# A two-layer attention and token-mixer kernel: the value column's ones on ScalarE, queries in front of keys, and three mixer rows in two parts

## The chip, the cores and the metric

One Trainium2 chip, of which the kernel uses one core. The metric is the device time of one execution in microseconds (us); smaller is better.

## What is computed

```python
x = A_x                                                        # 2048 tokens, D = 640
x = x + _A_ref(_layernorm(x), A_wqkv, A_wo)                    # layer 0: attention, 32 heads of 20
x = x + _B_ref(_layernorm(x), B_w1, B_b1, B_w2, B_b2)          # layer 0: token mixer
x = x + _A_ref(_layernorm(x), A_wqkv, A_wo)                    # layer 1, same weights
x = x + _B_ref(_layernorm(x), B_w1, B_b1, B_w2, B_b2)

# _A_ref: q, k, v = x @ wqkv; softmax(q k^T / sqrt(20)) v; @ wo
# _B_ref: u = gelu(einsum("bsd,sf->bdf", h, w1) + b1); y = einsum("bdf,fs->bds", u, w2) + b2
```

The mixer multiplies over the tokens: its first matrix w1 is 2048 x 1536, so every one of the 1536 rows of u needs all 2048 normalised tokens.

## The kernel before

**Tiles.** The 2048 tokens are 16 tiles of 128. Queries go in four blocks of 512 (tb or qb 0 to 3), heads in eight groups of four (g 0 to 7). Scores S are matmuls into PSUM (L703); ScalarE turns two or three banks of them at a time into exponentials P (L773), which is most of its work; PE multiplies P by the values (L1326, into acc). Vaug holds the values of each head with one more column of ones, so that the same matmul gives the softmax's sum; the column is written once, in layer 0's start (L1546, a VectorE memset of 128 x 512; the neighbouring padding is zeroed by ScalarE, L1544 to L1549). A part of the exponentials is worked out on VectorE (L563, L593, L597, L614, L616, with scores in the bank Dt and results in Pd), with steps of it on GpSimd (POOL: L661, L644).

**The order.** The program is written out by a planner in Python that runs when the kernel is built: `attention()` keeps an estimated clock for each engine, puts in score groups, attention x value matmuls and, in the room that is left on PE, fills, and the chip then runs each engine's instructions in this fixed order. A fill is a small group of matmuls with a priority (lowest first), and a step that empties its PSUM bank (misc or Dt): T transposes a normalised tile into hh (L1225, emptied at L366 on ScalarE or L370 on VectorE), V makes values (L1201), K and Q project keys and queries of one head group and one token block (L1177, emptied at L370 and L372), y is the mixer's second matmul of the layer in front (L1685, emptied at L1668), O the output projection (L1117), M the mixer's first matmul (L1068). Where no fill is there, matmuls of zeros stand (L762).

**Priorities in layer 1's front.** K of token block tb must come before the scores that use it; the four Q fills of block 1 follow with priority base[1] + 12 + 8g, behind K of their head groups.

**The mixer's first matmul.** The sum over token tiles is split into two groups, tiles 0 to 7 and 8 to 13; the last two tiles come at the end (um, L1753). `enqueue_mm1_partial` puts in, for each of the 12 rows ft of 128 features, two fills (columns 0 to 319 and 320 to 639) of eight or six matmuls. The first group's result goes by L1081 to ustg and by a DMA from POOL's queue to uacc in memory. For the second group (`direct`) `fetch_row` brings that row back (L1035) into buffers that have come free (three rows in a query buffer QTq, four in hh, five in KT), and L1076 adds the bank to it. The weight tile w1st of a row is loaded one row ahead (L1047, two buffers). The second group is put in when all of its tiles are normalised (`after` in `do_ln2`).

**The end of a layer.** `attention()` makes the rest of the attention x value matmuls, empties at most some fills into `tail_banks`, and calls `end_tiles`: residuals are copied into PSUM (L955), the gelu table is loaded (L956), the last output projection is added (L960), leftover fills follow, then the statistics and normalisation of tiles 14 and 15 (L980 to L999), then um. For layer 0 the next layer's front follows, for layer 1 the output tiles.

**The start of layer 0** (`TokenFeed.begin`). Tiles of x are loaded and normalised on VectorE (L886, L889, L893, L901, L907, with a power on POOL at L903), transposed, and copied on ScalarE (L366); ScalarE also copies the projection weights from w_raw into padded form (L1559).

Of the kernel before, what the change touches and what calls it, by code (L numbers as in the profile page):

```python
# [81 lines left out]
def kernel(  # L82
# [141 lines left out]
    def attention(st, x_in_ap, x_mid, uacc_l, feed, feed_stack):  # L224
# [705 lines left out]
        def do_ln2(tt, x1s, end):  # L930
            def dst():
                if tt >= IN_HH:
                    assert check_hT_dead()
                    h2_tiles[tt] = h2_view[:, tt, :]
                else:
                    assert len(vready) == 2 * NT
                    h2_tiles[tt] = h2_low[:, tt, :]
                return h2_tiles[tt]

            def after(e):  # L940
                ln_open.remove(tt)
                p = next(i for i, grp in enumerate(M_GROUPS) if tt in grp)
                if all(i in h2_tiles for i in M_GROUPS[p]):
                    enqueue_mm1_partial(p, e + DVE_TO_PE)
            ln_open.append(tt)
            ln_proc(x1s[:], True, dst, 3, end + DVE_NEXT, after)
# [74 lines left out]
        def fetch_row(ft):  # L1021
            if ft >= NF or ft in fetched:
                return
# [18 lines left out]

        def mm1_prefetch(p, ft):
            if ft < NF and (p, ft) not in w1_of:
                group = M_GROUPS[p]
                w1st = w1_of[(p, ft)] = late["w1sp"].tile([128, max(map(len, M_GROUPS)), 128], BF16, name="w1st")
                nc.sync.dma_start(out=w1st[:, 0:len(group), :],  # L1047
                                  in_=B_w1[group[0] * 128:(group[-1] + 1) * 128, ft * 128:(ft + 1) * 128].rearrange(
                                      "(a s) f -> s a f", s=128))

        def enqueue_mm1_partial(p, ready):
            group = M_GROUPS[p]
            rows_in = [h2_tiles[tt] for tt in group]
            n_in = len(group)
            direct = p == len(M_GROUPS) - 1
            rows = {}
            sent = {}

            mm1_prefetch(p, 0)
            for ft in range(NF):  # L1060
                for ci, (c0, c1) in enumerate(((0, D // 2), (D // 2, D))):
                    w = c1 - c0
                    mms = []
                    for sti in range(n_in):
                        def mm(t, sti=sti, ft=ft, c0=c0, c1=c1, w=w, ci=ci):
                            if sti == 0 and ci == 0:
                                mm1_prefetch(p, ft + 1)
                            pe(nc.tensor.matmul(t[:, 0:w], lhsT=w1_of[(p, ft)][:, sti, :],  # L1068
                                                rhs=rows_in[sti][:, c0:c1], start=(sti == 0), stop=(sti == n_in - 1)))
                            low_left[0] -= not direct and sti == n_in - 1  # L1070
                        mms.append(mm)
# [65 lines left out]
        def enqueue_outproj_last(half, pairs, ready):  # L1137
# [3 lines left out]
            if half == 0:  # L1141
                mm1_prefetch(1, 0)
                for ft in range(4):
                    fetch_row(ft)
# [72 lines left out]
        def t_fill(tt, h_bf, ready, done):  # L1217
# [15 lines left out]
            def after(end):  # L1233
# [3 lines left out]
                if all(4 * tb + i in tready for i in range(4)):  # L1237
# [9 lines left out]
                    if tb in EQ and tb > 0:  # L1247
                        for g in range(EG):
                            proj_fill("Q", g, tb, base[tb] + 16.0 + 8.0 * g - 4, at, fed=True)
                if len(tready) == NT and NQB > 1:  # L1250
# [24 lines left out]
        def fill_step(alloc=None):  # L1275
# [11 lines left out]
            if fs["idx"] == len(grp["mms"]):  # L1287
                t, bank = fs["tile"], fs["bank"]
                fs["cur"] = None
                eng = evac_engine() if grp["act"] else dvm  # L1290

# [161 lines left out]
        for t in sums:  # L1453
            zero_wave(t[:, 0:512], True, True)
            zero_wave(t[:, 512:D], True, True, HALF / 2, D - 512)
        tail_banks = [sums[0][:, 1024:1536], None, None]

        def tail_alloc():
            bank = tail_banks.pop()
            return bank if bank is not None else Dbank.alloc() if len(tail_banks) == 1 else misc.alloc()  # L1460
        room = pem["t"] + 1.3
# [9 lines left out]
    class TokenFeed:  # L1471
        groups = 4
        early_qbs = (0, 1)
        ve_early = True
        act_helps = True
        act_free = 0.0
# [29 lines left out]
        def begin(self, cx):  # L1506
# [36 lines left out]
            def zero_values(e):  # L1543
                nc.scalar.memzero(Vv[:, :, :, DH:VW])  # L1544
                nc.scalar.memzero(Vv[:, :, 4 * self.groups, 0:32 - VW])
                cx.submit(cx.Proc(2.6, [(0.49, lambda e: nc.vector.memset(Vv[:, :, :, DH:DH + 1], 1.0), 0.0)], e + 5.0))  # L1546
            cx.submit(cx.Proc(1.4, [(1.35, zero_values, -0.06),
                                    (0.2, lambda e: nc.scalar.memzero(Vaug[:, NKT * H * VW:]), -0.06)] +
                              [(1.0, lambda e, i=i: nc.scalar.memzero(pads(i, 1)), -0.06) for i in range(2)],  # L1549
                              2.1, eng=cx.acm))  # L1550

            def group_copy(i, g):
# [10 lines left out]
                def done(e):  # L1563
                    cx.w_at[(i, g)] = e + 0.05
                    self.second -= g >= self.groups
                ready = 22.0 if g >= self.groups else 11.0 if g else (6.2, 7.5)[i]
                cx.submit(cx.Proc((0 if g == 0 else 1.5) if g < self.groups else 5, [(0.5, copied, 0.0)], ready, eng=eng, after=done))
            for g in range(NG):
# [24 lines left out]
    class MixFeed:  # L1593
        groups = 4
        early_qbs = (0, 1)
        ve_early = False
        act_helps = True
        act_free = 0.0
# [284 lines left out]
```

## Time and profile before

| what | us |
|---|---|
| median of 3 runs (1754.08 to 1754.12) | 1754.12 |
| the profiled execution | 1754.05 |
| its span on the core | 1752.3 |
| first exponential starts | 15.97 |
| layer 0's last exponential ends, layer 1's first starts | 816.82, 853.26 |
| layer 1's last exponential ends | 1681.39 |

The span is the time from the first to the last recorded instruction. A timeline row gives start and duration in us, engine, line, operation, and in brackets the idle time before it and what ended it. A windows row gives a stretch, its length, the busy time with instruction count of each engine (or of one line), the granted clock as a share of full speed, the busy share of the DMA engines, and GB/s. A group row gives busy us, mean ns of one instruction, and the idle time in front. SP issues most of the DMAs, in order.

### The profile page before, as it was taken

To read this page: it belongs to the slowest core of one execution; us is meant where nothing else is said; L and a number is where in the kernel's file an instruction comes from. 1 tells how busy PE (TensorE), PEld (TensorE's weight loads), DVE (VectorE), ACT (ScalarE), POOL (GpSimd) and SP (SyncE) were. 2 spreads that over 40 slices of the span, in tenths; PEclk is the share of its full clock that TensorE was granted. 3 is DMA by queue.
4 is the path that set the end of the run, shared out by engine and by line. 5 is a ranking of instruction groups with operands and counts; after the bars stand their busy time and mean duration, and the time that the engine had idled before them with its cause. 6 is when DMAs were issued, how large, how long until landed. Compare 5 with 4: busy or idle time off the path is not lost.

```text
span 1752.3 us, 43289 instructions
## 1 busy us (share of the span) xinstructions
PE 1677.7 (96%) x17891; PEld 663.4 (38%) x17891; DVE 1534.9 (88%) x2491; ACT 1665.0 (95%) x1498; POOL 592.0 (34%) x936
## 2 busy tenths in 40 slices
PE   8999999999999999999999999999999999999999
PEld 3333333333333344444434433233333333444455
DVE  7789999999999999998543469999999999999973
ACT  8999999999999999999779999999999999999970
POOL 2243443353544343332000023434434443434310
PEclk9999999999999999999999999999999999999999
DMA  4020000000122010133322100001001220101445
GB/s 117 9 24 10 1 2 2 24 24 2 35 66 82 25 47 3 39 97 97 125 69 75 65 11 1 1 2 43 20 2 61 82 76 6 62 3 40 120 122 178
DMA packets 103014, 81.87 MB, mean 47 GB/s; under 512 B 50976, under 2 KB 87456, under 8 KB 102816
## 3 DMA queue, kind: packets, MB, share of 16 engines
q1 hardware_dynamic: 97280, 71.22, 13.5%
q0 software_dynamic: 5536, 7.88, 1.5%
q8 instruction: 140, 2.29, 0.5%
q14 instruction: 58, 0.48, 0.1%
HBM read 55.48 MB, written 23.59 MB: 45 GB/s over the span
## 4 chain that ended last, share of the span: by engine, by line
ACT 50%; PE 25%; issue 22%; DVE 2%; DMA 1%; POOL 0%; SPq 0%; ACTq 0%; DVEq 0%
ACT P L773 50%; PE S L703 7%; PE acc L1326 4%; PE misc L1068 2%; PE ya L1766 2%; PE misc L1177 2%; PE acc L762 2%; PE um L1753 1%; PE Dt L1177 1%; PE ya L1775 1%; PE yb L1766 1%; DMA w2s<-in_B_w_dram 1%; PE misc L1117 0%; PE misc L1685 0%; PE misc L1201 0%
## 5 line engine op out<-in xcount | busy, mean ns | idle before, releaser
L773 ACT ACTIVATE P<-S 128x1536 bf16<-128x1536 f32 (+1 forms) x1430 | 1617.4, 1369 | 13.5 <-PE S L703 13.0
L703 PE MATMUL S<-QTq,KT 32*128 32x512 bf16 (+1 forms) x4449 | 575.6, 337 | 60.9 <-ACT P L773 44.4
L661 POOL TENSOR_SCALAR ey<-ew 128x512 f16<-128x512 uint16 x516 | 320.6, 621 | 689.6 <-DVE et L597 306.4
L703 PEld LDWEIGHTS <-KT 32*128 32x128 bf16 x5127 | 229.6, 91 | 524.6 <-issue 497.0
L563 DVE TENSOR_SCALAR ew<-Dt 128x512 int32<-128x512 f32 x524 | 357.0, 681 | 22.3 <-PE Dt L703 14.8
L1326 PE MATMUL acc<-P,Vaug 128*32 128x512 bf16 (+1 forms) x4442 | 363.3, 343 | 0.3 <-DVE Vaug L370 0.3
L762 PE MATMUL acc<-zr,zw 128*32 128x512 bf16 x4256 | 328.1, 382 | 1.2 <-POOL zr L155 1.2
L597 DVE SCALAR_TENSOR_TENSOR et<-ey,ew 128x1024 int16<-128x1024 f16 x262 | 325.6, 1243 | 2.8
L644 POOL TENSOR_SCALAR Pd<-ew 128x512 int16<-128x512 int16 x317 | 196.8, 627 | 161.6 <-DVE et L597 42.4
L703 PE MATMUL Dt<-QTq,KT 32*128 32x512 bf16 (+1 forms) x678 | 201.4, 333 | 0.0
L593 DVE TENSOR_TENSOR ey<-ey 128x1024 f16<-128x1024 f16 x262 | 188.3, 719 | 1.4 <-POOL ey L661 0.3
L1326 PEld LDWEIGHTS <-Vaug 128*32 128x32 bf16 x5120 | 102.7, 94 | 175.4 <-issue 161.4
L762 PEld LDWEIGHTS <-zw 128*32 128x32 bf16 x4476 | 111.5, 96 | 97.9 <-issue 52.5
L616 DVE SCALAR_TENSOR_TENSOR Pd<-ew,et 128x1024 int16<-128x1024 int16 (+1 forms) x134 | 134.6, 1005 | 0.6
L614 DVE TENSOR_TENSOR Pd<-Pd,et 128x1024 int16<-128x1024 int16 (+1 forms) x189 | 121.8, 645 | 5.8 <-POOL Pd L644 3.8
L903 POOL TENSOR_TENSOR rstd<-veps,mhalf 128x1 f32<-128x1 f32 x60 | 49.4, 824 | 224.6 <-DVE veps L901 197.2
L1326 PE MATMUL acc<-Pd,Vaug 128*32 128x512 bf16 (+1 forms) x678 | 102.9, 336 | 1.4 <-DVE Pd L614 1.2
L1177 PE MATMUL misc<-hh,wq_pad 128*128 128x512 bf16 x290 | 84.0, 383 | 0.0
L1068 PEld LDWEIGHTS <-w1st 128*128 128x128 bf16 x672 | 52.9, 97 | 58.2 <-issue 45.3
L1177 PE MATMUL misc<-hh,wk_pad 128*128 128x512 bf16 x255 | 74.0, 383 | 0.0
L1068 PE MATMUL misc<-x1last,w1st 128*128 128x320 bf16 x384 | 73.0, 302 | 0.0
L1117 PE MATMUL misc<-wo_pad,attnT 128*128 128x320 bf16 x384 | 72.3, 302 | 0.2 <-DVE xin L1129 0.2
(145 smaller groups left out, 1180.4 us busy)
## 6 DMA issues: line engine op xcount, KB each, us to landing
w2s<-in_B_w_dram SPq DMA_DIRECT2D x16, 768.0 KB
uacc<-ustg POOLq DMA_DIRECT2D x24, 320.0 KB, 2.6
x1in<-xd SPq DMA_DIRECT2D x24, 320.0 KB
w1st<-in_B_w_dram SPq DMA_DIRECT2D x24, 256.0 KB
xd<-x2s SPq DMA_DIRECT2D x16, 320.0 KB
xin<-xd SPq DMA_DIRECT2D x16, 320.0 KB
w1st<-in_B_w_dram SPq DMA_DIRECT2D x24, 192.0 KB
xd<-x1s SPq DMA_DIRECT2D x12, 320.0 KB
```

Of the source, the lines that this page charges most:

```text
L563: nc.vector.tensor_scalar(out=w[:, slot, :], in0=Dt[:, :], scalar1=127.0 * FIX, scalar2=0.0, op0=ALU.add, op1=ALU.max)
L593: nc.vector.tensor_tensor(out=y, in0=y, in1=y, op=ALU.mult)
L597: nc.vector.scalar_tensor_tensor(out=box["t"][:, 0:512 * k], in0=ve_y.pop(p)[:, 0:512 * k], scalar=MANT_C * MANT_K ** 2, in1=frac, op0=ALU ...
L616: nc.vector.scalar_tensor_tensor(out=bits, in0=whole[:, lo:hi], scalar=128.0, in1=t, op0=ALU.mult, op1=ALU.add)
L644: after_vector(nc.gpsimd.tensor_scalar(out=bits, in0=whole, scalar1=128.0, scalar2=0.0, op0=ALU.mult, op1=ALU.add))
L661: return engine.tensor_scalar(out=out_ap, in0=in_ap, scalar1=MANT_K / FIX, scalar2=-MANT_K * MANT_S, op0=ALU.mult, op1=ALU.add)
L703: pe(nc.tensor.matmul(out_ap[:, c0:c0 + w], lhsT=KT[32 * j:32 * j + 32, g, kt * 128:(kt + 1) * 128], rhs=get_QT(st, qb)[32 * j:32 * j + 32 ...
L762: pe(nc.tensor.matmul(bank[32 * j:32 * j + 32, 0:w], lhsT=zw[:], rhs=zr[:, :, 0:64].to_broadcast([128, w // 64, 64]), start=start, stop=st ...
L773: nc.scalar.activation(out=P[:, 0:ncs, :].rearrange("p a b -> p (a b)"), in_=St[:, 0:ncs, :].rearrange("p a b -> p (a b)"), func=ACT.Exp, ...
L1068: pe(nc.tensor.matmul(t[:, 0:w], lhsT=w1_of[(p, ft)][:, sti, :], rhs=rows_in[sti][:, c0:c1], start=(sti == 0), stop=(sti == n_in - 1)))
L1177: pe(nc.tensor.matmul(t[:, :], lhsT=wpad[:, dt_, g, :], rhs=hT[:, dt_, tb * 512:(tb + 1) * 512], start=(dt_ == 0), stop=(dt_ == NDT - 1)))
L1326: pe(nc.tensor.matmul(acc[32 * j:32 * j + 32, a0:a0 + w], lhsT=Vaug[:, (kt * H + hh_) * VW:(kt * H + hh_) * VW + 32], rhs=P[:, slot, c0:c0 ...
```

## The change

Five edits. (1) In layer 0's start the ones of the value column are no longer a VectorE memset: ScalarE runs an ACTIVATE (identity with bias 1) over the column that it has just zeroed, between its own clearings; the planner's numbers for the pads and the weight copies change with it, and the copies of transposed tiles 0 to 3 are fixed to ScalarE (`act_evacs`). ScalarE's order becomes: zeros, ones, pads, copies of tiles 0 and 1, first key weights, tile 2, first query weights, tile 3, the other six weight copies (before: key weights, tile 0, query weights, tiles 1 to 3, six weight copies). (2) In layer 1 (`early_q`) the four query fills of block 1 get priority base[1] - 5.5, in front of that block's keys. (3) In layer 1 (`mid_rows = 3`) the second mixer group is put in as three parts: rows 0 to 2 with tiles 8 to 11 as soon as these exist, rows 3 to 11 with all six tiles, then rows 0 to 2 with tiles 12 and 13. That makes six more additions (L1076) and three more loads of w1st; the number of matmuls is the same. Layer 0 keeps one part. (4) `tail_alloc` goes round the banks misc, Dt and a score bank, and empties a waiting bank before it is used again. (5) `fetch_row` may not skip a row.

```diff
@@ -939,9 +939,13 @@
 
             def after(e):
                 ln_open.remove(tt)
-                p = next(i for i, grp in enumerate(M_GROUPS) if tt in grp)
-                if all(i in h2_tiles for i in M_GROUPS[p]):
-                    enqueue_mm1_partial(p, e + DVE_TO_PE)
+                if tt < IN_HH and all(i in h2_tiles for i in M_GROUPS[0]):
+                    enqueue_mm1(0, M_GROUPS[0], range(NF), e + DVE_TO_PE)
+                if IN_HH <= tt < 4 * LASTQB and feed.mid_rows and all(i in h2_tiles for i in M_GROUPS[1][:4]):
+                    enqueue_mm1(1, M_GROUPS[1][:4], range(feed.mid_rows), e + DVE_TO_PE)
+                if tt >= IN_HH and all(i in h2_tiles for i in M_GROUPS[1]):
+                    enqueue_mm1(2, M_GROUPS[1], range(feed.mid_rows, NF), e + DVE_TO_PE)
+                    enqueue_mm1(3, M_GROUPS[1][4:], range(feed.mid_rows), e + DVE_TO_PE)
             ln_open.append(tt)
             ln_proc(x1s[:], True, dst, 3, end + DVE_NEXT, after)
 
@@ -1019,7 +1023,7 @@
             return cursor[0] >= n
 
         def fetch_row(ft):
-            if ft >= NF or ft in fetched:
+            if ft >= NF or ft in fetched or ft > len(st.ua):
                 return
             if ft == len(st.ua):
                 if ft == 0:
@@ -1040,31 +1044,34 @@
                 fetch_row(ft + k)
             return ft in fetched and fetched[ft] <= pem["t"]
 
-        def mm1_prefetch(p, ft):
-            if ft < NF and (p, ft) not in w1_of:
-                group = M_GROUPS[p]
+        def mm1_prefetch(p, group, ft):
+            if (p, ft) not in w1_of:
                 w1st = w1_of[(p, ft)] = late["w1sp"].tile([128, max(map(len, M_GROUPS)), 128], BF16, name="w1st")
                 nc.sync.dma_start(out=w1st[:, 0:len(group), :],
                                   in_=B_w1[group[0] * 128:(group[-1] + 1) * 128, ft * 128:(ft + 1) * 128].rearrange(
                                       "(a s) f -> s a f", s=128))
 
-        def enqueue_mm1_partial(p, ready):
-            group = M_GROUPS[p]
+        def enqueue_mm1(p, group, fts, ready):
             rows_in = [h2_tiles[tt] for tt in group]
             n_in = len(group)
-            direct = p == len(M_GROUPS) - 1
+            direct = p > 0
             rows = {}
             sent = {}
-
-            mm1_prefetch(p, 0)
-            for ft in range(NF):
+            fts = list(fts)
+            if fts and p < 3:
+                mm1_prefetch(p, group, fts[0])
+            for fi, ft in enumerate(fts):
                 for ci, (c0, c1) in enumerate(((0, D // 2), (D // 2, D))):
                     w = c1 - c0
                     mms = []
                     for sti in range(n_in):
-                        def mm(t, sti=sti, ft=ft, c0=c0, c1=c1, w=w, ci=ci):
+                        def mm(t, sti=sti, fi=fi, ft=ft, c0=c0, c1=c1, w=w, ci=ci):
                             if sti == 0 and ci == 0:
-                                mm1_prefetch(p, ft + 1)
+                                mm1_prefetch(p, group, ft)
+                                if fi + 1 < len(fts):
+                                    mm1_prefetch(p, group, fts[fi + 1])
+                                elif p == 2 and feed.mid_rows:
+                                    mm1_prefetch(3, M_GROUPS[1][4:], 0)
                             pe(nc.tensor.matmul(t[:, 0:w], lhsT=w1_of[(p, ft)][:, sti, :],
                                                 rhs=rows_in[sti][:, c0:c1], start=(sti == 0), stop=(sti == n_in - 1)))
                             low_left[0] -= not direct and sti == n_in - 1
@@ -1139,7 +1146,7 @@
             tt0 = 4 * LASTQB + 2 * half
             load_xin(tt0)
             if half == 0:
-                mm1_prefetch(1, 0)
+                mm1_prefetch(2, M_GROUPS[1], feed.mid_rows)
                 for ft in range(4):
                     fetch_row(ft)
             for ttl in range(2):
@@ -1246,7 +1253,8 @@
                                       gate=feed.gate_late if g >= EG else None, fed=g < EG)
                     if tb in EQ and tb > 0:
                         for g in range(EG):
-                            proj_fill("Q", g, tb, base[tb] + 16.0 + 8.0 * g - 4, at, fed=True)
+                            proj_fill("Q", g, tb, base[tb] + (8.0 * g + 12.0 if feed.early_q is None else 0.01 * g + feed.early_q),
+                                      at, fed=True)
                 if len(tready) == NT and NQB > 1:
                     enqueue_qproj(1)
             add_fill(("T", tt), when(0, tb) - 6 + 0.1 * (tt % 4), mms, evac, D, ready=ready, after=after, wave=0.1,
@@ -1287,7 +1295,7 @@
             if fs["idx"] == len(grp["mms"]):
                 t, bank = fs["tile"], fs["bank"]
                 fs["cur"] = None
-                eng = evac_engine() if grp["act"] else dvm
+                eng = dvm if not grp["act"] else acm if grp["key"] in feed.act_evacs else evac_engine()
 
                 def emptied(end):
                     grp["evac"](t, end, eng)
@@ -1453,11 +1461,14 @@
         for t in sums:
             zero_wave(t[:, 0:512], True, True)
             zero_wave(t[:, 512:D], True, True, HALF / 2, D - 512)
-        tail_banks = [sums[0][:, 1024:1536], None, None]
+        tail_banks = [misc.alloc, Dbank.alloc, lambda: sums[0][:, 1024:1536]]
+        tail_used = [0]
 
         def tail_alloc():
-            bank = tail_banks.pop()
-            return bank if bank is not None else Dbank.alloc() if len(tail_banks) == 1 else misc.alloc()
+            if tail_used[0] >= len(tail_banks) and len(held) > 1:
+                force(held.pop(1))
+            tail_used[0] += 1
+            return tail_banks[(tail_used[0] - 1) % len(tail_banks)]()
         room = pem["t"] + 1.3
         while fs["cur"] is not None or (fill_queue and pem["t"] < room):
             fill_step(tail_alloc)
@@ -1472,6 +1483,9 @@
         groups = 4
         early_qbs = (0, 1)
         ve_early = True
+        act_evacs = [("T", tt) for tt in range(4)]
+        mid_rows = 0
+        early_q = None
         act_helps = True
         act_free = 0.0
         warm_until = 5.6
@@ -1543,10 +1557,11 @@
             def zero_values(e):
                 nc.scalar.memzero(Vv[:, :, :, DH:VW])
                 nc.scalar.memzero(Vv[:, :, 4 * self.groups, 0:32 - VW])
-                cx.submit(cx.Proc(2.6, [(0.49, lambda e: nc.vector.memset(Vv[:, :, :, DH:DH + 1], 1.0), 0.0)], e + 5.0))
             cx.submit(cx.Proc(1.4, [(1.35, zero_values, -0.06),
                                     (0.2, lambda e: nc.scalar.memzero(Vaug[:, NKT * H * VW:]), -0.06)] +
-                              [(1.0, lambda e, i=i: nc.scalar.memzero(pads(i, 1)), -0.06) for i in range(2)],
+                              [(0.55, lambda e: nc.scalar.activation(out=Vv[:, :, :, DH:DH + 1], in_=Vv[:, :, :, DH:DH + 1],
+                                                                     func=ACT.Identity, bias=1.0, scale=1.0), -0.06)] +
+                              [(0.5, lambda e, i=i: nc.scalar.memzero(pads(i, 1)), -0.06) for i in range(2)],
                               2.1, eng=cx.acm))
 
             def group_copy(i, g):
@@ -1563,8 +1578,8 @@
                 def done(e):
                     cx.w_at[(i, g)] = e + 0.05
                     self.second -= g >= self.groups
-                ready = 22.0 if g >= self.groups else 11.0 if g else (6.2, 7.5)[i]
-                cx.submit(cx.Proc((0 if g == 0 else 1.5) if g < self.groups else 5, [(0.5, copied, 0.0)], ready, eng=eng, after=done))
+                ready = 22.0 if g >= self.groups else 11.5 if g else (7.5, 8.7)[i]
+                cx.submit(cx.Proc((1.2 if g == 0 else 1.5) if g < self.groups else 5, [(0.5, copied, 0.0)], ready, eng=eng, after=done))
             for g in range(NG):
                 for i in range(2):
                     group_copy(i, g)
@@ -1592,8 +1607,11 @@
 
     class MixFeed:
         groups = 4
+        act_evacs = ()
         early_qbs = (0, 1)
         ve_early = False
+        mid_rows = 3
+        early_q = -5.5
         act_helps = True
         act_free = 0.0
         warm_until = 0.0
```

## The prediction

> **What bounds the kernel now.** I read the page first, then the windows of the exponentials' line alone, then the timelines around the holes. On the page a busy row gives us, share and count; a group's row gives busy us, mean ns, then idle time and its releaser.
>
> ```profile
> span 1752.3 us, 43289 instructions
> PE 1677.7 (96%) x17891; PEld 663.4 (38%) x17891; DVE 1534.9 (88%) x2491; ACT 1665.0 (95%) x1498; POOL 592.0 (34%) x936
> L773 ACT ACTIVATE P<-S 128x1536 bf16<-128x1536 f32 (+1 forms) x1430 | 1617.4, 1369 | 13.5 <-PE S L703 13.0
> ```
>
> PE has the larger share, but part of it is L762, which multiplies zeros; the exponentials wait only 13.5 us in all. Windows of L773 (stretch, its length, busy us) and ScalarE's timeline (start, us):
>
> ```profile
> 15.97:816.82 800.85, 800.28 (x707) 1.00 0.12 32
> 853.26:1681.39 828.13, 817.11 (x723) 1.00 0.13 40
> 1681.39:1752.30 70.91, 0.01 (x1) 1.00 0.59 182
> ```
>
> ```profile
> 883.44 7.37 ACT L773 ACTIVATE P<-S 128x1024 bf16<-128x1024 f32 x7 [8.34 <-PE S L703]
> 892.16 7.38 ACT L773 ACTIVATE P<-S 128x1536 bf16<-128x1536 f32 x7 [1.35 <-PE S L703]
> 900.59 6.88 ACT L773 ACTIVATE P<-S 128x1024 bf16<-128x1024 f32 x6 [1.05 <-PE S L703]
> ```
>
> So time can go only where ScalarE is not exponentiating: the start (15.97), the middle (853.26 - 816.82 = 36.44), the end (70.91), and 828.13 - 817.11 = 11.02 of holes in layer 1, of which 8.34 + 1.35 + 1.05 = 10.74 are these three. Layer 0 has 0.57. The changed program's order equals the old one on PE until the first projection of key block 1 in layer 1 (889.48); so the middle and the 8.34 stay. The sum is made against the profiled run, 1754.05: span 1752.3 and 1.75 around it. The median of the runs is 1754.12.
>
> **1. The start.** VectorE, then ScalarE:
>
> ```profile
> 10.06 0.48 DVE L1546 MEMSET Vaug<- 128x512 bf16 x1 [1.90 <-ACT hh L366]
> 10.14 0.55 DVE L907 TENSOR_SCALAR h_bf<-x0in,mv,rstd 128x640 bf16<-128x640 bf16 x1
> 10.61 0.48 DVE L886 BATCH_NORM_STATS2 bnst<-x0in 128x6 f32<-128x320 bf16 x1
> 14.63 0.68 DVE L372 TENSOR_SCALAR QTq<-misc 128x512 bf16<-128x512 f32 x1
> ```
>
> ```profile
> 2.12 1.10 ACT L1544 ACTIVATE Vaug<-Vaug 128x1024 uint32<-128x1024 uint32 x1
> 3.13 0.24 ACT L1545 ACTIVATE Vaug<-Vaug 128x64 uint32<-128x64 uint32 x1
> 7.60 0.53 ACT L1559 COPY wk_pad<-w_raw 128x400 bf16<-128x400 bf16 x1 [3.15 <-DMA w_raw<-in_A_wqkv_dram]
> ```
>
> VectorE stood 1.90 in front of the memset, and then ran without a real gap to the query cast at 14.63, from which the first scores start. The memset goes, so normalised tile 3 may be made before 10. But the chain that ends in 14.63 begins with the statistics of tile 4 at 10.61, and that needs the tile. Windows across the loads (all engines; the last three numbers are clock, DMA share, GB/s):
>
> ```profile
> 10.00:10.40 0.40, 0.19 (x4) 0.00 (x0) 0.34 (x2) 0.40 (x1) 0.00 (x0) 1.00 0.94 320
> 10.40:10.80 0.40, 0.05 (x1) 0.05 (x2) 0.40 (x3) 0.04 (x1) 0.00 (x0) 1.00 0.61 221
> ```
>
> The queues are full until 10.4 and thin out behind it, so I take the tile to be there at about 10.45: the gain is 10.61 - 10.45 = **0.15**, not 1.90. Late next is the load, and nothing on ScalarE. Ends: 1.2, if the tile is there long before (the chain then starts behind tile 3, which is ready about 1.2 earlier), and a loss, as follows. The new ScalarE instruction is not in the trace. From 64 and 1024 elements (0.24, 1.10) 512 cost 0.24 + 448/960 x 0.86 = 0.64. It lies in the 3.15 us in which ScalarE waits for the weights, so I take nothing; without that cover, 0.64 lost. The first copies of transposes already ran on ScalarE; they only move ahead of weight copies, which wait for that load.
>
> The Trainium skill, "ScalarE: Activation LUTs", section "Rules for kernel authors", gives simple adds to VectorE and so speaks against this move; its section "What ACT_TABLE_LOAD costs" would make the instruction 186 + 0.833 x 512 = 613 ns (an estimate), against 480 in the memset's row. By that rule the start loses 0.13 instead of gaining 0.15; the 3.15 us of idle speak against its applying here.
>
> **2. Queries in front of keys.** PE around the two smaller holes:
>
> ```profile
> 889.48 1.24 PE L1177 MATMUL misc<-hh,wk_pad 128*128 128x512 bf16 x5
> 890.56 0.84 PE L1201 MATMUL Dt<-wv,hh 128*128 128x320 bf16 x5
> 891.67 0.60 PE L703 MATMUL S<-QTq,KT 32*128 32x512 bf16 x5
> ...
> 898.18 0.37 PE L703 MATMUL S<-QTq,KT 32*128 32x512 bf16 x1
> 898.49 0.82 PE L1177 MATMUL misc<-hh,wk_pad 128*128 128x512 bf16 x3
> 899.14 1.03 PE L1177 MATMUL Dt<-hh,wk_pad 128*128 128x512 bf16 x4
> 900.11 0.60 PE L703 MATMUL S<-QTq,KT 32*128 32x512 bf16 x5
> ```
>
> Five projection matmuls take 890.56 - 889.48 = 1.08, 0.216 each. At the first hole the new order has five query matmuls where five key ones stood, then four more (0.86), then the scores; before there were five value matmuls and four of attention x value, 891.67 - 890.56 = 1.11. So the scores come 1.11 - 0.86 = **0.25** earlier; ends 0 and 1.35. The second hole came from seven key matmuls in a row between two scores (898.49 to 900.11, 1.62 us). In the new order at most five projections stand between two score groups there (1.08), and score groups of two or three alternate throughout: I take the whole **1.05**; ends 0 (the block is only moved; keys now come later) and 1.05. No DMA moves. Queries are cast by VectorE like the keys (0.68 at L372), with no new wait.
>
> **3. One exponential fewer** for the same columns: by the 64 and 1024 rows an instruction's fixed part is 0.24 - 64 x 0.0009 = 0.18, of which back-to-back issue hides much (2.12 + 1.10 against 3.13); I take **0.05**, ends 0 and 0.18.
>
> **4. The end.** PE in layer 1, then layer 0's counterparts:
>
> ```profile
> 1682.33 0.72 PE L1068 MATMUL misc<-hh,w1st 128*128 128x320 bf16 x4
> 1683.85 0.97 PE L1068 MATMUL misc<-hh,w1st 128*128 128x320 bf16 x6 [0.81 <-DVE KT L1076]
> 1684.66 1.25 PE L960 MATMUL S<-wo_pad,attnT 128*128 128x512 bf16 x8
> 1689.30 1.25 PE L1753 MATMUL um<-hh,KT 128*128 128x512 bf16 x8 [0.30 <-ACT hh L995]
> ```
>
> ```profile
> 823.27 1.25 PE L1753 MATMUL um<-hh,KT 128*128 128x512 bf16 x8 [0.25 <-DMA wv<-in_A_wqkv_dram]
> ```
>
> Before, mixer matmuls were left over when attention ended: one group had to wait for VectorE to empty the bank and held L960 to 1684.66. From the last exponential to the first um this took 1689.30 - 1681.39 = 7.91. Layer 0 has nothing left over there: 823.27 - 816.82 = 6.45. The new order has nothing left over in layer 1 either, and the same sequence as layer 0's: 7.91 - 6.45 = **1.46**; ends 0 (another wait ends last) and 0.81 + 0.97 = 1.78. What follows um is the same program.
>
> **5. The split itself.** Three rows get an early part of four tiles and a late part of two. Matmuls stay the same in number; they replace zeros. Six additions of 320 columns come to VectorE and six small weight loads to SP (27 instead of 24, the same bytes). Each addition waits for a row of partial sums (two per row), fetched earlier than before:
>
> ```profile
> uacc<-ustg POOLq DMA_DIRECT2D x24, 320.0 KB, 2.6
> L563 DVE TENSOR_SCALAR ew<-Dt 128x512 int32<-128x512 f32 x524 | 357.0, 681 | 22.3 <-PE Dt L703 14.8
> L597 DVE SCALAR_TENSOR_TENSOR et<-ey,ew 128x1024 int16<-128x1024 f16 x262 | 325.6, 1243 | 2.8
> L614 DVE TENSOR_TENSOR Pd<-Pd,et 128x1024 int16<-128x1024 int16 (+1 forms) x189 | 121.8, 645 | 5.8 <-POOL Pd L644 3.8
> 1680.43 0.48 DVE L1076 TENSOR_TENSOR KT<-Dt,KT 128x320 f32<-128x320 f32 x1
> ```
>
> A row of that size lands some 2.6 us after issue; an x row is issued ahead of it on SP. In VectorE's new order eight operations of exponential chunks stand between the release of the first fetch and the first addition: two L563, two L597, two L614 and two L593 (median 683, below), 2 x (0.681 + 1.243 + 0.645 + 0.683) = 6.5. So the row is there and I take nothing. Without the cover every chunk behind it waits, then attention x value on PE, then scores. Weight tiles: a row's load is issued when the row before the last has left its buffer, and more than 150 PE instructions lie between; nothing.
>
> The six additions are 6 x 0.48 = 2.9 us. VectorE's free time (third pair of numbers; windows, and L593's own durations):
>
> ```profile
> 1260.00:1460.00 200.00, 191.91 (x1839) 69.93 (x1838) 195.04 (x295) 200.00 (x178) 82.87 (x135) 1.00 0.16 49
> 1460.00:1681.00 221.00, 214.68 (x3293) 94.93 (x3296) 215.43 (x335) 220.98 (x197) 83.41 (x128) 1.00 0.15 46
> L593 DVE TENSOR_TENSOR ey<-ey x262: 622/683/1092, 60.2 to 1676.5; 128x1024 f16<-128x1024 f16 x131
> ```
>
> 5.0 and 5.6 us are free, and ScalarE is full in both. The new order also gives POOL 16 more Pd steps and 4 fewer ey steps, which takes eight steps of L616 from VectorE. I take nothing; the price is rival C.
>
> **Sum:** 0.15 + 0.25 + 1.05 + 0.05 + 1.46 = 2.96; 1754.05 - 2.96 = **1751.1**, 0.17% less. 0.2% (3.5 us; about what a measurement of this kernel can tell from no change) is not reached: below 1750.6 counts as faster, above 1757.6 as slower.
>
> **Rivals.**
> A, more at the start: tile 4 is there early and the 1.2 comes whole: 1754.05 - 1.2 - 2.81 = 1750.0. For it speaks the idle 1.90, against it the full queues.
> B, it doesn't do what it says: the 1.90 wasn't the memset's, and the holes of layer 1 only move, since delayed keys need the same PE time: 1.46 + 0.05 remain, 1752.5. For it: all key matmuls are still to be done before block 1. Against: they are spread.
> C, slower: VectorE becomes the bound in layer 1. The twelve more POOL steps can each hold an operation with two SBUF inputs (L593 ranges from 622 to 1092, so up to 0.47), 5.6 us, with the 2.9 of the additions 8.5. What doesn't find idle time comes back as holes in L773: all of it gives 1759.6, half 1755.4. It decides from the point where the 5 us of a window are used up, or don't lie where the additions fall. Against it: the eight L616 go. The Trainium skill, "Advanced Engine Details and Errata", section "VectorE Performance Modes", says that POOL and VectorE share a port and block each other; the spread of L593 agrees.
>
> **Chances.** Forecast 0.57, A 0.23, B 0.10, C 0.10 (0.07 of it above 1757.6). Faster 0.25 (A, and the forecast's edge), same 0.68, slower 0.07. Range: the best ends of 2, 3 and 4 with 0.15 at the start give 1754.05 - 0.15 - 1.35 - 1.05 - 0.18 - 1.78 = 1749.5, which takes in A; the worst, 0.64 lost and all gains 0, give 1754.7. Most of C is left out.
>
> **What would show it.** Right: first exponential near 15.8; no hole of 1.05 near 900, one of about 1.1 near 892; 6.45 from the last exponential to um; holes elsewhere in layer 1 under 0.5 together. Wrong: the first exponential near 14.8 (A); new holes behind 889 (B); VectorE waiting for QTq rows, or PE for Pd with ScalarE idle (C).

## The result and the profile after

| | before | changed |
|---|---|---|
| median of 20 runs each, us | 1754.13 | 1751.11 |
| ratio, with 95% interval | | 0.9982 (0.9976 to 0.9989) |
| lowest and highest run | 1754.01, 1755.55 | 1750.41, 1752.8 |
| profiled run, its span | 1754.05, 1752.3 | 1751.01, 1748.9 |

The change makes the kernel 3.0 us faster, 0.18%; the interval lies wholly below 1. Its runs spread more widely. Windows of the exponentials (L773) in the changed kernel, up to the first one, layer 0, the middle, layer 1, and the rest:

```profile
0.00:15.70 15.70, 0.00 (x1) 1.00 0.69 204
15.70:816.54 800.84, 800.28 (x707) 1.00 0.12 32
816.54:852.98 36.44, 0.00 (x1) 1.00 0.59 194
852.98:1679.66 826.68, 816.80 (x722) 1.00 0.13 40
1679.66:1748.90 69.24, 0.00 (x0) 1.00 0.60 187
```

Against before: start 0.27 shorter, layer 0 and the middle equal, layer 1 828.13 - 826.68 = 1.45 shorter, the rest 70.91 - 69.24 = 1.67 shorter; 3.4 of span. The time outside the span went from 1.75 to 2.11, so 3.04 is left. In layer 1, ScalarE's timeline has two holes where there were three:

```profile
883.16 7.37 ACT L773 ACTIVATE P<-S 128x1024 bf16<-128x1024 f32 x7 [8.34 <-PE S L703]
891.74 28.62 ACT L773 ACTIVATE P<-S 128x1536 bf16<-128x1536 f32 x25 [1.20 <-PE S L703]
```

The stretch that begins at 891.74 runs past 900, where the hole of 1.05 was. PE there has the nine query matmuls at the first hole (the first row counts four, but its 1.24 is the time of five, and the weight loads of that stretch are nine: one record is missing). Up to 901 it then never has more than four query or key matmuls between score groups:

```profile
889.20 1.24 PE L1184 MATMUL misc<-hh,wq_pad 128*128 128x512 bf16 x4
890.28 1.03 PE L1184 MATMUL Dt<-hh,wq_pad 128*128 128x512 bf16 x4
891.24 0.60 PE L703 MATMUL S<-QTq,KT 32*128 32x512 bf16 x5
...
898.99 1.04 PE L1184 MATMUL misc<-hh,wk_pad 128*128 128x512 bf16 x4
900.01 0.39 PE L703 MATMUL S<-QTq,KT 32*128 32x512 bf16 x3
```

At the end no mixer matmul follows the last scores; from the last exponential (1679.66) to um it takes 6.44:

```profile
1681.21 0.43 PE L964 MATMUL S<-wo_pad,attnT 128*128 128x512 bf16 x2 [0.56 <-ACT S L959]
1681.95 0.76 PE L964 MATMUL S<-wo_pad,attnT 128*128 128x128 bf16 x5 [0.32 <-DVE attnT L834]
1682.65 3.21 PE L762 MATMUL acc<-zr,zw 128*32 128x512 bf16 x56
1686.10 1.25 PE L1771 MATMUL um<-hh,KT 128*128 128x512 bf16 x7 [0.25 <-ACT hh L999]
```

In the start, VectorE no longer stands before a memset but before tile 4, whose load releases its statistics (10.31), and ScalarE's new instruction is long (first VectorE, then ScalarE):

```profile
8.80 0.45 DVE L907 TENSOR_SCALAR h_bf<-x0in,mv,rstd 128x640 bf16<-128x640 bf16 x1 [0.67 <-POOL rstd L903]
10.31 0.49 DVE L886 BATCH_NORM_STATS2 bnst<-x0in 128x6 f32<-128x320 bf16 x1 [1.06 <-DMA x0in<-in_A_x_dram]
```

```profile
3.37 2.54 ACT L1562 ACTIVATE Vaug<-Vaug 128x512 bf16<-128x512 bf16 x1
5.40 0.92 ACT L1564 ACTIVATE wk_pad<-wk_pad 128x480 uint32<-128x480 uint32 x1
6.88 0.69 ACT L366 COPY hh<-misc 128x640 bf16<-128x640 bf16 x1
```

### The profile page after: what moved, and what is told of

It is laid out like the page before. It is cut to its first block, busy times and chain, and to the rows that moved or that the text cites. A ratio compares the mean times of both kernels' runs of the same rounds, so it can differ in the third digit from the quotient of the medians.

```text
span 1748.9 us, 43173 instructions
## 1 busy us (share of the span) xinstructions
PE 1666.2 (95%) x17767; PEld 664.3 (38%) x17848; DVE 1538.9 (88%) x2502; ACT 1666.9 (95%) x1498; POOL 599.6 (34%) x948
## 4 chain that ended last, share of the span: by engine, by line
ACT 51%; PE 25%; issue 22%; DVE 1%; DMA 0%; SPq 0%; another core or an unknown queue 0%; POOL 0%; ACTq 0%; DVEq 0%
ACT P L773 51%; PE S L703 7%; PE acc L1334 4%; PE ya L1784 2%; PE misc L1075 2%; PE acc L762 2%; PE misc L1184 2%; PE um L1771 1%; PE Dt L1184 1%; PE ya L1793 1%; PE yb L1784 1%; PE misc L1124 0%; PE Dt L1703 0%; PE misc L1208 0%; PE misc L1703 0%
## 5 line engine op out<-in xcount | busy, mean ns | idle before, releaser
L773 ACT ACTIVATE P<-S 128x1536 bf16<-128x1536 f32 (+1 forms) x1429 | 1617.1, 1373 | 13.5 <-PE S L703 13.1
L597 DVE SCALAR_TENSOR_TENSOR et<-ey,ew 128x1024 int16<-128x1024 f16 x262 | 326.0, 1244 | 2.8
L762 PE MATMUL acc<-zr,zw 128*32 128x512 bf16 x4184 | 324.6, 382 | 1.2 <-POOL zr L155 1.2
L644 POOL TENSOR_SCALAR Pd<-ew 128x512 int16<-128x512 int16 x333 | 206.8, 626 | 168.4 <-DVE et L597 44.7
L614 DVE TENSOR_TENSOR Pd<-Pd,et 128x1024 int16<-128x1024 int16 (+1 forms) x197 | 129.8, 659 | 5.5 <-POOL Pd L644 3.3
L616 DVE SCALAR_TENSOR_TENSOR Pd<-ew,et 128x1024 int16<-128x1024 int16 (+1 forms) x126 | 123.5, 980 | 0.6
L1184 PE MATMUL misc<-hh,wq_pad 128*128 128x512 bf16 x255 | 75.8, 383 | 2.8 <-issue 1.6
```

The costliest lines, as they stand in the source:

```text
L597: nc.vector.scalar_tensor_tensor(out=box["t"][:, 0:512 * k], in0=ve_y.pop(p)[:, 0:512 * k], scalar=MANT_C * MANT_K ** 2, in1=frac, op0=ALU ...
L614: nc.vector.tensor_tensor(out=bits, in0=bits, in1=t, op=ALU.add)
L644: after_vector(nc.gpsimd.tensor_scalar(out=bits, in0=whole, scalar1=128.0, scalar2=0.0, op0=ALU.mult, op1=ALU.add))
L762: pe(nc.tensor.matmul(bank[32 * j:32 * j + 32, 0:w], lhsT=zw[:], rhs=zr[:, :, 0:64].to_broadcast([128, w // 64, 64]), start=start, stop=st ...
L773: nc.scalar.activation(out=P[:, 0:ncs, :].rearrange("p a b -> p (a b)"), in_=St[:, 0:ncs, :].rearrange("p a b -> p (a b)"), func=ACT.Exp, ...
L1184: pe(nc.tensor.matmul(t[:, :], lhsT=wpad[:, dt_, g, :], rhs=hT[:, dt_, tb * 512:(tb + 1) * 512], start=(dt_ == 0), stop=(dt_ == NDT - 1)))
```

## The experiments

Theory: the three parts act at separate places, and each keeps its gain alone. Rivals: the parts depend on each other; VectorE pays for the split; the start's 1.90 us belonged to the place and not to the memset. Each run below was timed 11 times beside 33 runs of before (medians 1754.24, 1754.18 and 1754.21 in the three sets).

### Each part alone

The switches of the changed kernel, one part on at a time (start_only has the first part as in the diff above):

```diff
 class MixFeed:                 # start_only   queries_only   rows_only
-        mid_rows = 3           # 0            0              3
-        early_q = -5.5         # None         -5.5           None
 class TokenFeed:               # as changed   as before      as before
```

> The kernel before with the start's edit alone (ones of the value column on ScalarE, copies of tiles 0 to 3 fixed to ScalarE); PE's order is that of before. Theory (the parts are separate and each acts at its own place): the first exponential at 15.70 as with the whole change, 0.28 earlier, all else as before: 1753.8, and the runs as close together as before's (0.3). Rival (the start's gain is a chance of when the tile lands, not of the edit): first exponential anywhere between 15.7 and 16.0 and no gain in the median. If the 0.36 that the whole change has more outside the span belongs to the start, it shows here: 1754.1.

> The kernel before with the four queries of block 1 in front of that block's keys in layer 1, alone. Theory: the hole of 1.05 near 899.5 is gone, that of 1.35 near 890.8 is 1.2, nothing comes in their place: 1754.13 - 1.2 = 1752.9; from the last exponential to um it stays 7.9. Rival (the holes only move, and the rows' split is what fills them): holes in layer 1 add up to 11.0 as before, 1754.1. The whole change's wider spread (2.4 between its runs against 0.3 for nearly all of before's) may come with this part's other order of VectorE and POOL: then it shows here.

> The kernel before with the three rows in two parts in layer 1 (and the bank order at the end), alone. Theory: nothing is left over at the end, 6.45 from the last exponential to um instead of 7.91; both holes near 891 and 899.5 stay; VectorE's six more additions cost nothing: 1754.13 - 1.5 = 1752.6. Rival (VectorE pays for them): new holes of 0.5 to 3 in L773 behind 1460, 1753.2 or more. If the spread of the whole change comes from here, the runs spread over 2 us.

> The changed kernel once more, beside its parts. Theory (separate parts): 0.3 + 1.2 + 1.5 = 3.0 below before, 1751.1; the three parts alone add up to it within 0.4. Rival (they help or hinder each other): the sum of the parts is off by over 0.7. The spread again about 2 us, and 2.1 outside the span where before has 1.75.

| | median | ratio (95%) | first exponential to last | last exponential to um |
|---|---|---|---|---|
| before | 1754.24 | | 1665.42 | 7.91 |
| start_only | 1753.96 | 0.9999 (0.9990 to 1.0008) | 1665.46 | 7.91 |
| queries_only | 1755.27 | 1.0005 (0.9996 to 1.0013) | 1663.63 | 10.63 |
| rows_only | 1753.24 | 0.9994 (0.9986 to 1.0003) | 1666.20 | 6.42 |
| all_parts | 1751.13 | 0.9981 (0.9972 to 0.9990) | | |

(The profiled run of all_parts fell on a lower clock, of which below; the changed kernel's profile has 1663.96 and 6.44.) The theory of separate parts fell. (The intervals of single parts reach over 1; but the runs of queries_only lie from 1754.96 to 1756.17, where most of before's lie from 1754.1 to 1754.5, those of rows_only from 1753.08 to 1753.90 but for one of 1757.23, and the profiles show where it goes.) The three medians alone add up to 0.28 - 1.03 + 1.00 = 0.25 of gain, together they give 3.1. start_only's runs spread from 1753.24 to 1755.83, not within the 0.3 that I expected. Edits 4 and 5 are in all of these programs; start_only, whose end takes before's 7.91, shows that they cost nothing there by themselves.

Something else differs between these programs, which the planner decides: how many chunks of 1024 columns of exponentials go to VectorE (one L597 each). In layer 1 these are 122 before and in the changed kernel, 121 in rows_only, 123 in queries_only. Windows of L773 in layer 1, rows_only, then queries_only:

```profile
853.35:1682.24 828.89, 817.89 (x724) 1.00 0.13 40
853.59:1679.90 826.31, 816.21 (x721) 1.00 0.13 40
```

Against before's 817.11, ScalarE's exponentials last 0.78 longer in rows_only and 0.90 less in queries_only. rows_only's holes are 11.00 in all, as before's 11.02, so that it misses the expected 1752.6 by the chunk, and not by waits for VectorE. In the sum of the parts the two chunks nearly cancel.

The queries do what they should in the front: the hole of 1.05 is gone alone too, and the exponentials are through 1.79 earlier, about half of it from holes and half from the chunk (ScalarE):

```profile
892.34 18.18 ACT L773 ACTIVATE P<-S 128x1536 bf16<-128x1536 f32 x16 [1.21 <-PE S L703]
```

But um comes later. PE at the end of queries_only; its last exponential ends at 1679.90, so all of this lies between that and um:

```profile
1682.54 0.98 PE L1075 MATMUL misc<-hh,w1st 128*128 128x320 bf16 x6 [1.21 <-DVE KT L1083]
1683.36 0.98 PE L1075 MATMUL Dt<-hh,w1st 128*128 128x320 bf16 x6
1684.17 1.25 PE L964 MATMUL S<-wo_pad,attnT 128*128 128x512 bf16 x7
1685.26 0.98 PE L1075 MATMUL S<-hh,w1st 128*128 128x320 bf16 x6
1686.07 0.98 PE L1075 MATMUL misc<-hh,w1st 128*128 128x320 bf16 x6
...
1690.53 1.25 PE L1770 MATMUL um<-hh,KT 128*128 128x512 bf16 x7 [1.21 <-ACT hh L999]
```

Four mixer groups stand there, against the rest of one and two whole ones before. The room between scores in which they would have run has become shorter with the attention; that this is why they are left is my reading of the order, not shown apart. They cost in two places. L964 begins 4.27 behind the last exponential, where it was 3.27. And VectorE has to empty a leftover group's bank S in front of the statistics, and waits for it:

```profile
1686.33 0.49 DVE L1083 TENSOR_TENSOR KT<-S,KT 128x320 f32<-128x320 f32 x1 [1.47 <-PE S L1075]
1686.74 0.89 DVE L984 BATCH_NORM_STATS2 bnst<-S 128x6 f32<-128x320 f32 x2
```

So from L964 to um it takes 6.36 instead of 4.64. Whether edit 4's order of banks puts it there wasn't tried. With the split, three rows have most of their work done some 70 us earlier (their partial sums are fetched at 1522.20 instead of 1591.37), where zeros were multiplied before: 4476 zero matmuls before, 4464 in queries_only, 4408 in the changed program. So the split's worth isn't only the 1.46 of leftover work that I saw in before; it is also what lets the queries keep their gain.

### Queries and rows without the start

```diff
 class MixFeed:
-        early_q = None
+        early_q = -5.5          # on rows_only
```

> The kernel before with queries in front and rows in two parts, without the start's edit. Theory (the queries' gain of 1.2 is lost at the end when mixer work is left over there, five groups alone, and kept when the split has put that work earlier): nothing left over, 6.4 from the last exponential to um, 1754.24 - 2.8 = 1751.4; the runs lie within 0.3 but for those with a lower clock, since the memset hides when tile 4 lands. Rival (the parts only add up): 1754.24 - 1.0 + 1.0 = 1754.2.

1751.91 (ratio 0.9988, 0.9979 to 0.9997), first exponential 15.96, 1664.48 to the last and 6.45 to um. Against -1.03 + 1.00 alone this is 2.3 faster: the two belong together. It misses the 1751.4 by 0.5: in the same order of exponentials it falls behind the changed kernel in layer 1 in small steps, about one for 64 of them, 0.52 in all. queries_only falls behind the same order with the start's edit (no_rows, below) by 0.55 from the first exponential to the last, while start_only and before differ by 0.04 only. So the start's edit brings some 0.5 in layer 1 where the queries stand in front; why isn't settled.

### How many rows have to be split

```diff
 class MixFeed:
-        mid_rows = 3
+        mid_rows = 0            # no_rows; 1: one_row; 6: six_rows
```

> The changed kernel with no row split (start and queries alone). Thirty matmuls of the mixer stand behind the last scores, against 19 before and none in the changed kernel. Theory (the front's gain comes back as leftover work at the end): holes near 899.5 gone, but 10.4 to 10.8 from the last exponential to um, 1755.0. Rival (it was a fault of the queries alone run): 6.5 to 8 to um, 1752.5.

> The changed kernel with one row split instead of three; eight mixer matmuls stand behind the last scores. Theory (what stays over is paid only as far as it reaches past the time that the end waits anyway): between 6.45 and 7.5 to um, 1751.1 to 1752.0. Rival (each split row is worth its share of the 4 us): about 9.2 to um, 1753.7.

> The changed kernel with six rows split instead of three: twelve more additions than before on VectorE instead of six, nothing left over in either. Theory (VectorE hides them and there is nothing more to gain): 1751.1, 6.45 to um, holes behind 1460 under 0.3 together. Rival (VectorE is at its bound): new holes of 1 to 3 in L773, 1752 to 1754.

Medians 1754.52 (no rows), 1751.04 (one), 1751.11 (three, above) and 1751.17 (six). Without the split um starts 10.63 after the last exponential, as in queries_only:

```profile
1689.07 1.25 PE L1771 MATMUL um<-hh,KT 128*128 128x512 bf16 x8 [1.21 <-DMA x1in<-xd]
```

With one row 7.54 stand there, but the exponentials are through 0.9 earlier; from the first exponential to um it is 1670.6, with three rows 1670.4, with none 1673.7, before 1673.3. The 7.54 lies just outside the 7.5 that I allowed. As built, then, one row does as well as three, and more than three give nothing. But the 0.9 is again a chunk that the planner gave to VectorE (123 of them with one row, as with none; 122 with three and with six):

```profile
853.05:1678.82 825.77, 815.82 (x721) 1.00 0.13 40
```

At equal chunks one row would be about 1.0 behind three by these two profiles (816.80 - 815.82 = 0.98; an estimate, not a run). Six rows, with twice the additions, cost nothing either: the medians of one, three and six rows lie within 0.13. Its profile fell on a lower clock; behind the hole near 891 it has none over 0.2 in layer 1. The rival that VectorE pays fell. VectorE has more free time in the changed kernel than before (219.60 - 211.09 = 8.5 us, against 5.6):

```profile
1460.00:1679.60 219.60, 212.46 (x3231) 95.37 (x3229) 211.09 (x332) 219.58 (x195) 87.64 (x136) 1.00 0.17 47
```

### What the memset cost

```diff
-nc.vector.memset(Vv[:, :, :, DH:DH + 1], 1.0)                    # before
+nc.vector.memset(Vv[:, :, :, DH:DH + 2].bitcast(U32), 16256)     # wide_ones, on before
-nc.scalar.activation(out=Vv[:, :, :, DH:DH + 1], ..., bias=1.0)             # changed
+nc.scalar.activation(out=Vv[:, :, :, DH:DH + 2].bitcast(U32), ..., bias=16256.0)  # wide_act
```

16256 is the bit pattern of a bf16 one in the lower half and a zero, which belongs there, in the upper.

> The kernel before, in which the memset of the ones stays on VectorE at its place, but writes 512 elements of 4 bytes (the one and the zero behind it) instead of 512 of 2 bytes. Theory (the 1.90 of idle time is the memset's own: single 2-byte elements 48 bytes apart take about 4 ns each, on ScalarE 2.54 us for the same 512): no idle time in front of it, it is over by 8.8, tile 4's statistics then wait for the tile as without the memset: first exponential between 15.2 and 16.1 from run to run, median 1753.9, runs spread over 1 us or more. Rival (VectorE stands at this place for another reason): 1.9 of idle time at about 10.05 as before, runs within 0.3 of 1754.2.

> The changed kernel with ScalarE's ones as 512 elements of 4 bytes instead of 2. Theory (width): the instruction takes 0.6 instead of 2.54, the first copy of a transposed tile starts near 5.5 instead of 6.88, and the time stays, since tile 4's landing sets the start: 1751.1, spread as the changed kernel. Rival (2.54 is the cost of writing there while the loads run): 2.5 again. If the copies were late because of it, 1750.6 or less.

VectorE in wide_ones:

```profile
8.64 0.48 DVE L1547 MEMSET Vaug<- 128x512 uint32 x1 [0.44 <-ACT wq_pad L1560]
8.96 0.34 DVE L908 TENSOR_SCALAR h_bf<-x0in,mv,rstd 128x640 bf16<-128x640 bf16 x1
9.72 0.49 DVE L887 BATCH_NORM_STATS2 bnst<-x0in 128x6 f32<-128x320 bf16 x1 [0.41 <-DMA x0in<-in_A_x_dram]
```

The idle 1.90 has become 0.44 and tile 3 follows at 8.96 instead of 10.14: the rest was the memset's own, though the row booked it as a wait for ScalarE. 1753.82 against 1754.18, about what moving it to ScalarE brings (1753.96 against 1754.24); neither is clear of noise, and both spread alike. On ScalarE the 4-byte form takes 1.13 where the 2-byte form took 2.54, not the 0.6 I expected, and the time stays at 1751.07. So width is most of the cost; that these 512 elements take as long as the 1024 in pairs (1.10) isn't explained by it, and wasn't tried further. The pads are then cleared 1.3 earlier, but the copy of tile 0 begins at the same time, since it waits for PE:

```profile
3.38 1.13 ACT L1563 ACTIVATE Vaug<-Vaug 128x512 uint32<-128x512 uint32 x1
...
6.85 0.69 ACT L367 COPY hh<-misc 128x640 bf16<-128x640 bf16 x1 [1.35 <-PE misc L1233]
```

### What the start waits for

```diff
-            load_w(self.wv[:, 0], 2 * D)
             for tt in range(4, 6):
                 load_x(tt)
+            load_w(self.wv[:, 0], 2 * D)       # x_first; best has wide_act too
```

> The changed kernel with one thing moved: the loads of x tiles 4 and 5 are issued in front of the value weights instead of behind them. Theory (the landing of tile 4 sets the first exponential): tile 4's statistics start near 9.2 instead of 9.8 to 10.7, the first exponential at 14.6 to 15.1, 1750.3, and the runs lie closer together. Rival (the value weights, now about 0.5 us later, hold the value matmuls that stand in front of the first keys on PE): first exponential near 15.7 or later, 1751.1 or more.

> The changed kernel with x tiles 4 and 5 loaded in front of the value weights and ScalarE's ones as 4-byte elements. Theory (the value weights now hold the start, not ScalarE): as with the loads alone, first exponential at 14.6 to 15.4, 1750.7. Rival (ScalarE's copies are the next to end last): first exponential 0.4 earlier still, 1750.3.

In x_first tile 4's statistics begin at 9.10, right behind tile 3; then PE waits for the value weights (they lie in the buffer x1last), and the first exponential starts at 14.79. VectorE, PE:

```profile
9.10 0.49 DVE L886 BATCH_NORM_STATS2 bnst<-x0in 128x6 f32<-128x320 bf16 x1
```

```profile
10.17 0.85 PE L1208 MATMUL misc<-x1last,hh 128*128 128x320 bf16 x5 [0.48 <-DMA x1last<-in_A_wqkv_dram]
```

So tile 4's landing did set the start, and the value weights are next. The medians are 1750.76 (x_first) and 1750.78 (best), some 0.35 below the changed kernel's 1751.11, which lies within what runs of 11 tell apart; I had expected 1750.3 and a narrower spread for x_first. The spread (1750.0 to 1751.93) stays; whether the landing of the value weights now makes it isn't shown. best's first exponential is at 14.90, not earlier than x_first's, so ScalarE wasn't the next to end last.

## Why the prediction was right, point by point

The total was forecast as 1751.1 and came as 1751.11. That it fits so closely is luck: in the profiled run the parts are 0.27 + 1.14 + 0.31 + 1.47, and 0.20 - 0.36 that stood nowhere in the sum, 3.03 together against 2.96. What held is the mechanism of the end and of the second hole, in the whole program.

- **Start, 0.15:** 0.27 in the profiled run. The mechanism held (the tile's landing takes over), but not as one number, and 0.15 was near by chance. In the eight profiles with the loads in the old order and without the narrow memset, tile 4's statistics began between 9.69 and 11.20, and the first exponential each time 5.38 or 5.39 behind them (15.70 in the changed kernel, 16.03 in all_parts, 15.23 in start_only). Before, the memset's end covered this, except where the tile came later still (queries_only: 10.90, first exponential 16.27); that is one source of the spread. The 1.90, which the working read as a wait, was mostly the memset's own, as wide_ones shows. The 0.64 for ScalarE's instruction was a quarter of the real 2.54. The working took the slope from rows whose elements are 4 bytes, neighbours in pairs; this one touches single 2-byte elements 48 bytes apart. The cover of 3.15 just held. The rule against this move from the Trainium skill, "ScalarE: Activation LUTs", "Rules for kernel authors", didn't decide, because of that cover; its formula's 613 ns, too, is a quarter of what the run shows.
- **Queries, 0.25 + 1.05:** 0.15 + 1.05 in the profile, less 0.06 of other small holes. As a price of the edit it was wrong: alone, the queries cost 1.0. I read both holes off the order of the whole changed program, in which the split is contained. The step that failed is to add up the queries' and the rows' gains as separate terms, which exist only together.
- **One exponential fewer, 0.05:** L773 was busy 816.80 instead of 817.11, 0.31. But queries_rows, with the same 722 exponentials, has 817.19, so the term isn't shown; the 0.31 may be part of the open 0.5 above.
- **End, 1.46:** 7.91 - 6.44 = 1.47. Reading it off layer 0, where nothing is left over, was sound.
- **Split, nothing:** right as a cost, and six rows confirm it. VectorE didn't wait for the fetched rows.
- **Not in the sum:** 0.20 less between um and the end of the span, and 0.36 more outside the span. The 0.36 is there in every profile with the changed order and three rows (2.1 in all), and not in programs with one, six or no rows or one part alone (about 1.75), so it goes with one program and not with a step of the work; its cause is open.

Rival A (1.2 at the start) came true in part, in runs whose tile landed early. Rival B came about only where the queries were changed without the rows, and in another way than I wrote: the holes don't move, the work does. Rival C didn't.

**The wider spread.** Besides the tile's landing there is a second source, which before has too. Of the changed kernel's 31 runs, all over 1751.8 but one have a mean clock of 0.999, and the profile of all_parts caught one of these (that of six_rows another, at the same place). Windows of all engines (PE first, clock third from the end), then of PE alone, with a stretch of the changed kernel's own profile as the last row, then ScalarE's hole:

```profile
886.00:888.00 2.00, 1.81 (x14) 1.03 (x14) 0.91 (x2) 2.00 (x2) 0.00 (x0) 0.81 0.00 0
888.00:889.00 1.00, 1.00 (x6) 0.13 (x4) 0.08 (x1) 1.00 (x2) 0.00 (x0) 0.50 0.00 0
889.00:890.00 1.00, 1.00 (x11) 0.14 (x8) 0.00 (x0) 0.80 (x2) 0.00 (x0) 0.50 0.00 0
890.00:891.00 1.00, 1.00 (x7) 0.35 (x5) 0.05 (x1) 1.00 (x2) 0.00 (x0) 0.67 0.07 16
```

```profile
880.38:883.80 3.42, 3.42 (x29) 1.00 0.74 201
883.80:887.21 3.41, 2.55 (x26) 1.00 0.62 233
883.41:886.82 3.41, 2.55 (x27) 1.00 0.67 248
```

```profile
893.29 6.88 ACT L773 ACTIVATE P<-S 128x1536 bf16<-128x1536 f32 x6 [1.99 <-PE S L703]
```

From 887.2 to 890.7, 3.4 us, PE ran at half speed, right in front of the nine query matmuls, and the hole of 1.20 became 1.99 + 0.20. In the 3.4 us before, in which it transposes and waits for ScalarE, PE was busy for 2.55. The changed kernel's profile has such a stretch with the same 2.55, and its clock stayed at 1.00 behind it; so the busy time alone doesn't decide. The Trainium skill, "TensorE: Matmul & The Clock Gate", section "What's actually happening", says that the clock is halved after a window of 3413 ns with too little activity and that these windows run freely. The length and the 0.50 agree. By it the lower clock would depend on where the windows fall, and so on when the run starts; that only some runs have it (a mean clock of 0.999 in 7 of the changed kernel's 31 and in 14 of before's 99 in the three sets) fits, but this wasn't tried.

## What to carry to other kernels

When two engines are both nearly full, a hole closed on one is only worth something if the other's work still finds room; test edits alone and together before giving each a price, and look for what has come to stand behind the last wave. Work that can be started in part as soon as part of its inputs are there is a cheap filler: here three rows of twelve left nothing over. Where a planner shares out the work, look for what it moved besides the edit before comparing parts. And look at the idle time in front of an instruction as possibly its own cost, above all where it writes single narrow elements far apart.

## What the runs showed of the hardware

Writing 512 bf16 values 48 bytes apart took ScalarE 2.54 us, the same places as 4-byte elements 1.13 (0.24 for 64 and 1.10 for 1024 paired 4-byte elements, before). On VectorE the 2-byte memset stood for 1.90 us in front of its own 0.48, and as 4-byte elements for 0.44, part of which may be something else. The profile gives such time to the idle time in front and names as its releaser whatever ended about then: ScalarE's copy of a tile in one run, its copy of weights in another (1.88).
